# Retention attention on one core: the products across chunks done for two pairs of heads at a time

## Chip, core and metric

The kernel runs on one core of one Trainium2 chip. The metric is the device time in microseconds (us) of one execution; lower is better.

## What is computed

The program is a retention layer followed by two feed-forward layers, all in float32.

```python
# attention: B, H, S, D = 4, 8, 576, 64
scores = scale * (q @ k.T)                     # per batch and head
gamma = 1.0 - 2.0 ** (-5.0 - np.arange(H))
Dmat = np.where(rel >= 0, gamma[:, None, None] ** rel, 0.0)   # rel = row - column
x = (scores * Dmat) @ v                        # -> 2304 tokens x 512
# two layers, 512 -> 2048 -> 512
h = x @ w_in;   g = max(h, 0) + alpha * min(h, 0);   x = g @ w_out
h = x @ w2_in;  g = h * sigmoid(1.702 * h);          out = g @ w2_out
```

## The kernel before

Two heads are worked on together and called a pair: 4 batches times 4 pairs give 16 pairs, numbered 0 to 15 in `PAIRS`. The 64 rows of the first head lie on partitions 0 to 63, those of the second on 64 to 127 (`halves`). The 576 positions are cut into four chunks of 128 and a tail of 64. Because the decay is a power of the distance, the result of a chunk has two parts: a product within the chunk (a masked score matrix times v), and a product across chunks (a decayed 64x64 running state times the queries of the chunk).

The attention is a loop with one round per pair and one more at the end (`for i in range(n_a + 1)`). The program order on every engine is the order of this code; nothing moves instructions later. The PE work of round i is, in this order:

- `a_scores(i)`: k times q per chunk, K = 64 rows, one head on each half of the array's rows; results in `sc`.
- `a_outer(i)`: k times v per chunk, all 128 rows, one head on each half of the array's columns; results in `st`.
- `a_within(j)` with j = i - 1: the masked scores times v, again one head on each half of the columns; results in `av`.
- `a_tail(i)`: the scores of the 64-position tail, 64x64, one head on each of two tiles on the diagonal of the array; results in `st`.
- `a_across(j)`: the states times the queries, 64x64 tiles, one head on each of the two diagonal tiles: three chunks of 128 columns, one of 64, and the "corner" that uses the tail's scores. It adds to `av`.

Beside it the other engines do the following for each pair. DVE: `a_evac(i)` multiplies the two score tiles by a decay table into `r` (L319); `a_sums(i)` makes three small running sums of states (L348, L353, L358); `a_rests` forms the low part of x, for pairs 0 to 7 alone (L91, x<-av). ACT: `a_states(i)` scales `st` into `r` (L251), `a_keys(i+1)` scales the keys in `kts` (L251), and `a_out(j)` copies `av` out (L86, into `x` or `xs`). POOL: `a_queries(i)` scales the queries. SP issues the loads: `a_load(i+4)` at the end of round i fetches the 864 KB of a pair's q, k and v into `ld` (L243), and 256 KB of keys in another layout into `kts` (L245). There are five `ld` buffers, so the load of pair n waits until pair n - 5 has been read for the last time, which is the corner product in `a_across`.

Between these steps the loop also prepares the first layer's weights, from a table of times (`rows`, `at`, `run_to`): for each of the first three blocks of weights two loads of 512 KB on SP (L115), and on DVE a clamp, two bit operations and a subtraction (L123, L126, L133, L140, L91 w<-cv). After the attention come the first layer (L445, L488) and the second (L613).

In PSUM, `av` has two buffers of two banks, `sc` three of one, `st` one.

Of the kernel before, what the change touches and what calls it, by code (L numbers as in the profile page):

```python
# [26 lines left out]
TMP = {"ld": (4, 5, 6, 7, 10), "r": (8, 9), "xs": (12, 13, 14, 15)}  # L27
A0 = 256
# [13 lines left out]
def kernel(  # L42
# [42 lines left out]
    def copy(out, in_):  # L85
        return nc.scalar.activation(out=out, in_=in_, func=ACTF.Copy)  # L86
# [12 lines left out]
    def run_to(time):  # L99
        while events and events[0][0] <= time:  # L100
            _, _, fn, args = events.pop(0)
            fn(*args)
# [122 lines left out]
                at(tick(t + max(d + 2.4, 5.2) + 1.3), b_store, j, i)  # L225


    ld, r_t, k_t, s_t, sc_t, av_t, xs_t = {}, {}, {}, {}, {}, {}, {}

    def tmp(what, i, shape):  # L230
        tags = TMP[what]
        return wp.tile(shape, F32, tag=f"w{tags[i % len(tags)]}", name=what)

    halves = (slice(0, 64), slice(64, 128))
    def kts(i):
        return kts_t[i // 4 % 2][:, i % 4]

    def a_load(i):
        b, p = PAIRS[i]
        t = tmp("ld", i, [128, 1728])  # L240
# [14 lines left out]
        return fade_sb[o, c:c + n]  # L255

    def a_decay():
        dq = aps.tile([128, 1024], F32, tag="av", name="dq", bufs=2)
        for c in range(0, H * 128, 512):
            nc.tensor.matmul(  # L260
                out=dq[:, c:c + 512], lhsT=ones, rhs=fades_sb[:, c:c + 512], start=True, stop=True,
                skip_group_check=True,
            )
        for c in range(0, H * 128, 512):
            copy(fade_sb[:, c:c + 512], dq[:, c:c + 512])

    def a_tables(p):
        def table(o, c0, n, row, key):
# [28 lines left out]
    def a_scores(i, chunks=range(4)):  # L297
# [4 lines left out]
        for j in chunks:  # L302
            for e, o in enumerate(halves):
                mm(t[e][:, j * 128:j * 128 + 128], k[j][o], q[j][o], j == 0, True)

    def a_tail(i):
        q, k = ld[i][0:2]
        for o in halves:
            mm(s_t[i][o, 0:64], k[4][o], q[4][o], i == 0, True)

    def a_outer(i):
        t, v, n = s_t[i], ld[i][2], k_t.pop(i)
        for j in range(4):
            for e, o in enumerate(halves):
                mm(t[o, j * 64 + 64:j * 64 + 128], n[:, j, o], v[:, 2 * j + e], i > 0 and j == 0, True)

    def a_evac(i):
        for e, t in enumerate(sc_t.pop(i)):
            nc.vector.tensor_tensor(  # L319
                out=r_t[i][0][:, e].rearrange("p (j n) -> p j n", j=4),  # L320
                in0=t.rearrange("p (j n) -> p j n", j=4),
                in1=tab_sb[:, PAIRS[i][1], e * 128:e * 128 + 128].rearrange(
                    "p (a n) -> p a n", a=1).to_broadcast([128, 4, 128]),
                op=ALU.mult,
            )

    def a_queries(i):
        behind = latest[0]
        r = tmp("r", i, [128, 2048])
        r_t[i] = (  # L330
            r[:, 0:1024].rearrange("p (e n) -> p e n", e=2), r[:, 1024:1536],
            r[:, 1088:1600].rearrange("p (b n) -> p b n", b=2)[:, :, 0:64], r[:, 1600:2048],
        )
# [27 lines left out]

    def a_within(i):
        v, r = ld[i][2], r_t[i][0]
        t = aps.tile([128, 1024], F32, tag="av", name="av", bufs=2)
        av_t[i] = t, [t[:, A0 + j * 128:A0 + j * 128 + 128] for j in range(4)] + [t[:, A0 + 512:A0 + S]]
        for j in range(4):
            for e, o in enumerate(halves):
                mm(av_t[i][1][j][o], v[:, 2 * j + e], r[:, e, j * 128:j * 128 + 128], j % 2 == 0, True)

    def a_across(i):  # L370
        out, v = av_t[i][1], ld[i][2]
        _, s, _, q = r_t.pop(i)
        for c in range(1, 5):
            s0 = 64 if c == 1 else 192 + c * 64
            for o in halves:
                mm(out[c][o], s[o, s0:s0 + 64], q[o, c * 128 - 128:min(c * 128, 448)], False, True)
        for o in halves:
            mm(out[4][o], v[o, 8], s[o, 0:64], False, True)

    def a_out(i):  # L380
        b, p = PAIRS[i]
        t = av_t.pop(i)[0][:, A0:A0 + S]
        ld.pop(i)
        s0 = 0
        for c in range(2):
            n0, n1 = max(CH[c][0] - b * S, 0), min(CH[c][1] - b * S, S)
            if n0 >= n1:
                continue
            if (0, c, p) not in x_t:
                x_t[0, c, p] = xp[c].tile([128, 2, 512], F32R, tag=f"x{p}", name="x")  # L390
            o = b * S - CH[c][0]
            x = x_t[0, c, p][:, :, n0 + o:n1 + o]
            copy(x[:, 0], t[:, n0:n1])
            rests.append((x, t[:, n0:n1]))
            s0 = n1
        if s0 < S:
            n = i - NP
            if n // 3 not in xs_t:
                xs_t[n // 3] = tmp("xs", n // 3, [128, 3, S])
            copy(xs_t[n // 3][:, n % 3, s0:S], t[:, s0:S])  # L400

    rests = []

    def a_rests():
        while rests:
            x, t = rests.pop(0)
            sub(nc.vector, x[:, 1], t, x[:, 0])

    def a_store(i):
        b, p = PAIRS[i]  # L410
        s0, n = 448 if b == 1 else 0, i - NP
        nc.sync.dma_start(out=x0[b][:, p, s0:S], in_=xs_t[n // 3][:, n % 3, s0:S])


    g_t = {}
# [331 lines left out]

    with tc.manual_schedule():
        kts_t = [wp.tile([128, 4, 512], F32, tag=f"w{n}", name="kts") for n in (3, 11)]
        for t, a in ((fades_sb, fades), (vtab_sb, vtab)):  # L750
            nc.scalar.dma_start(out=t, in_=a)
        nc.vector.memset(wz, 0.0)  # L752
# [19 lines left out]
        a_otab(0)  # L772
        for i in range(n_a + 1):
            j = i - 1
            if i < n_a:
                a_scores(i)
                a_queries(i)
                a_evac(i)
            if i in (1, 2):
                a_tables(i + 1)  # L780
            a_rests()
            run_to(i)
            if i < n_a:
                s_t[i] = aps.tile([128, 512], F32, tag="st", name="st")
                if i == 0:
                    a_tail(i)
                    a_fill(1)
                a_outer(i)
                if i == 0:
                    a_states(i)  # L790
                    a_tables(1)
            if i != 1:
                a_within(max(j, 0))
            if 0 < i < n_a:
                a_tail(i)
                a_states(i)
            if i < n_a:
                a_sums(i)
            if i + 1 < n_a:
                a_keys(i + 1)  # L800
            if i == 0:
                a_otab(1)
# [138 lines left out]
def _layout(q, k, v, moe_w_in, moe_w_out, moe_alpha, moe2_w_in, moe2_w_out):  # L941
# [59 lines left out]
```

## Time and profile before

| | us |
|---|---|
| median of 3 runs | 818.18 (817.46 to 818.82) |
| the profiled execution, its own time | 817.99 |
| its span | 816.3 |
| PE busy in the span | 811.8 |
| DVE busy in the span | 629.1 |
| ACT busy in the span | 461.3 |

The span runs from the first instruction to the last; the execution's own time has 1.7 us more around it. PE is busy for 99% of the span. That does not say that every part of it is at the same limit: the attention is the first 68 us, the rest is the two layers.

### The profile page before, as it was taken

How to read it: one execution, taken by the hardware profiler on the slowest of the kernel's cores; microseconds unless marked ns; L12 is line 12 of the kernel's file. 1: busy time of each engine (PE TensorE's matmuls, PEld its weight loads, DVE VectorE, ACT ScalarE, POOL GpSimd, SP SyncE). 2: the span in 40 equal slices, each digit the busy share in tenths (PEclk: the TensorE clock that was granted, in tenths of full speed). 3: DMA queues.
4: the chain of work that ended last, by engine and by line, in shares of the span. 5: the costliest groups of instructions: out<-in, count | busy, mean ns of one | idle time of the engine just before them, and what ended most of it. 6: DMA issues, size and time to landing. Idle time of an engine off the chain costs nothing.

```text
span 816.3 us, 14024 instructions
## 1 busy us (share of the span) xinstructions
PE 811.8 (99%) x5102; PEld 743.0 (91%) x5102; DVE 629.1 (77%) x1145; ACT 461.3 (57%) x927; POOL 36.6 (4%) x54
## 2 busy tenths in 40 slices
PE   9999999999999999999999999999999999999998
PEld 8988888888888888999888899999999999999998
DVE  6897877786665778687579888699687799677775
ACT  6666655545344544554455766576566666566553
POOL 2330000000001010100100000000000000000000
PEclk9999999999999999999999999999999999999999
DMA  9994734443265665664566553877544986446871
GB/s 348 395 337 158 238 129 154 155 155 129 99 218 183 202 210 185 220 208 155 169 192 194 179 164 110 312 276 275 176 120 139 350 295 226 141 123 208 301 265 70
DMA packets 65722, 166.61 MB, mean 204 GB/s; under 512 B 7155, under 2 KB 32755, under 8 KB 59894
## 3 DMA queue, kind: packets, MB, share of 16 engines
q1 hardware_dynamic: 60896, 148.93, 53.0%
q0 software_dynamic: 4608, 16.78, 7.1%
q8 instruction: 40, 0.66, 0.3%
q14 instruction: 28, 0.23, 0.1%
q10 hardware_dynamic: 150, 0.02, 0.0%
HBM read 128.48 MB, written 37.22 MB: 203 GB/s over the span
## 4 chain that ended last, share of the span: by engine, by line
PE 99%; DVE 0%; issue 0%
PE h L445 24%; PE acc L488 24%; PE acc L613 24%; PE h L613 19%; PE av L287 4%; PE sc L287 2%; PE st L287 2%; PE wps L764 0%; PE dq L260 0%; DVE c L516 0%; DVE wz L752 0%
## 5 line engine op out<-in xcount | busy, mean ns | idle before, releaser
L445 PE MATMUL h<-x,w 128*128 128x512 f32 (+1 forms) x960 | 210.6, 368 | 0.0
L488 PE MATMUL acc<-gsf,w 128*128 128x512 f32 (+1 forms) x960 | 209.8, 368 | 0.0
L86 ACT ACTIVATE gsf<-g 128x384 fp32r<-128x384 f32 (+2 forms) x248 | 132.9, 543 | 116.7 <-DVE g L457 73.8
L445 PEld LDWEIGHTS h<-x,w 128*128 128x128 f32 x960 | 168.1, 189 | 30.8 <-ACT xs L86 0.4
L488 PEld LDWEIGHTS acc<-gsf,w 128*128 128x128 f32 x960 | 168.3, 189 | 30.0
L91 DVE TENSOR_TENSOR gsf<-g,gsf 128x384 fp32r<-128x384 f32 (+2 forms) x248 | 141.3, 578 | 49.0 <-ACT gsf L86 48.4
L457 DVE SCALAR_TENSOR_TENSOR g<-h,nalpha_sb,g 128x512 f32<-128x512 f32 (+1 forms) x80 | 55.6, 695 | 66.8 <-ACT h L456 66.7
L613 PE MATMUL acc<-x,ws 128*128 128x384 f32 x552 | 106.8, 334 | 0.0
L613 PE MATMUL acc<-gsf,ws 128*128 128x384 f32 x576 | 101.3, 334 | 0.0
L613 PEld LDWEIGHTS acc<-gsf,ws 128*128 128x128 f32 x576 | 100.0, 188 | 0.0
L613 PEld LDWEIGHTS acc<-x,ws 128*128 128x128 f32 x552 | 96.7, 188 | 0.0
L613 PE MATMUL h<-x,ws 128*128 128x384 f32 x456 | 90.3, 334 | 0.0
L455 ACT ACTIVATE g<-h 128x512 f32<-128x512 f32 (+1 forms) x80 | 43.8, 548 | 69.9 <-PE h L445 69.9
L613 PEld LDWEIGHTS h<-x,ws 128*128 128x128 f32 x456 | 80.1, 188 | 0.1
L613 PE MATMUL h<-gsf,ws 128*128 128x384 f32 x432 | 76.4, 334 | 0.0
L613 PEld LDWEIGHTS h<-gsf,ws 128*128 128x128 f32 x432 | 75.0, 188 | 0.1
L516 DVE TENSOR_TENSOR tm<-h,tm 128x384 f32<-128x384 f32 x73 | 40.5, 554 | 32.2 <-PE h L613 27.6
L91 DVE TENSOR_TENSOR ws<-rw,ws 128x512 fp32r<-128x512 f32 x96 | 56.9, 615 | 0.0
L516 DVE TENSOR_TENSOR g<-g,g 128x384 f32<-128x384 f32 x93 | 51.4, 552 | 0.7
L86 ACT ACTIVATE ws<-rw 128x512 fp32r<-128x512 f32 x96 | 49.8, 569 | 0.2 <-DMA rw<-rg 0.2
L456 ACT ACTIVATE h<-h 128x512 f32<-128x512 f32 (+1 forms) x80 | 43.9, 549 | 0.0
L119 ACT ACTIVATE cv<-raw 128x1024 f32<-128x1024 f32 x32 | 36.4, 1136 | 6.7 <-DMA raw<-in_w_dram 5.5
(83 smaller groups left out, 712.5 us busy)
## 6 DMA issues: line engine op xcount, KB each, us to landing
ws<-sg SPq DMA_DIRECT2D x42, 1024.0 KB, 6.4
raw<-in_w_dram SPq DMA_DIRECT2D x32, 512.0 KB, 4.9
raw<-in_w_dram POOLq DMA_DIRECT2D x32, 512.0 KB, 5.3
rw<-rg SPq DMA_DIRECT2D x24, 512.0 KB, 3.6
ld<-in_qkv_dram SPq DMA_DIRECT2D x13, 864.0 KB, 7.0
rw<-rg SPq DMA_DIRECT2D x24, 384.0 KB, 3.1
sg<-sums SPq DMA_DIRECT2D x40, 128.0 KB, 2.3
kts<-in_kn_dram SPq DMA_DIRECT2D x16, 256.0 KB, 7.1
```

Of the source, the lines that this page charges most:

```text
L86: return nc.scalar.activation(out=out, in_=in_, func=ACTF.Copy)
L91: latest[0] = eng.tensor_tensor(out=out, in0=a, in1=b.bitcast(F32), op=ALU.subtract)
L119: nc.scalar.activation(out=cvs[key], in_=raws[key][:, :, 1].bitcast(F32), func=ACTF.Abs)
L287: return nc.tensor.matmul(out=out, lhsT=lhsT, rhs=rhs, start=start, stop=stop, skip_group_check=True)
L445: nc.tensor.matmul(out=t, lhsT=w[:, cw, k * 128:k * 128 + 128], rhs=x[:, cx], start=(i == 0), stop=(i == 3 * NK - 1),)
L455: nc.scalar.activation(out=g, in_=t, func=ACTF.Relu)
L456: nc.scalar.activation(out=t, in_=t, func=ACTF.Relu, scale=-1.0)
L457: nc.vector.scalar_tensor_tensor(out=g, in0=t, scalar=nalpha_sb[:, m:m + 1], in1=g, op0=ALU.mult, op1=ALU.add)
L488: nc.tensor.matmul(out=acc[0][d], lhsT=w[:, cw, d * 128:d * 128 + 128], rhs=g[:, cx], start=(m == m0 and i == 0), stop=(m == m1 - 1 and i ...
L516: nc.vector.tensor_tensor(out=out, in0=x, in1=y, op=op)
L613: nc.tensor.matmul(out=out, lhsT=w(cw), rhs=x(cx), start=(start and n == 0), stop=True, skip_group_check=True,)
```

## The change

- `a_across` takes two pairs at once, 2m and 2m+1, and is called in every second round (even i, for pairs i - 2 and i - 1). For odd pairs the output halves are swapped (`side`): the first head's result goes to partitions 64 to 127, the second's to 0 to 63. With that the four heads of two pairs lie on four different 64x64 tiles of the array.
- So that the first layer still sees the right rows, the weight rows of odd 128-row blocks of `w_in` are rolled by 64 when the arrays are laid out.
- PSUM is dealt out anew: `av` is one bank for each of an even and an odd pair (the four chunks), the 64-column tail of the result has its own tile `avt` (one bank for the even pair; the odd pair takes one of the three `sc` banks), and `st` has two banks.
- `a_tail` for pairs 2m and 2m+1 is done in one place, in round 2m. So the tail of an odd pair now reads its `ld` a round earlier than anything did before.
- `a_keys(i+1)` moves ahead of `a_outer(i)`, and so on ACT ahead of `a_states(i)`.
- `a_out` of two pairs follows each `a_across`, with the 64-column tail as a copy of its own. `a_rests` of the even pair stands ahead of `a_evac` in the odd round, that of the odd pair behind it.
- The homes of `r` and `xs` in SBUF are laid out differently, since two more pairs are alive at a time. The number of `ld` buffers stays five, and SP's transfers are the same in the same order.

```diff
+    def side(i, e):
+        return halves[(e + i) % 2]
...
     def a_within(i):
         v, r = ld[i][2], r_t[i][0]
-        t = aps.tile([128, 1024], F32, tag="av", name="av", bufs=2)
-        av_t[i] = t, [t[:, A0 + j * 128:A0 + j * 128 + 128] for j in range(4)] + [t[:, A0 + 512:A0 + S]]
+        t = av_t[i] = aps.tile([128, 512], F32, tag=f"av{i % 2}", name="av")
         for j in range(4):
+            for e in range(2):
+                mm(
+                    t[side(i, e), j * 128:j * 128 + 128], v[:, 2 * j + e],
+                    r[:, e, j * 128:j * 128 + 128], j == 0, True,
+                )
+
+    def a_across(pair):
+        for i, tag, bufs in zip(pair, ("av2", "sc"), (1, 3)):
+            t = aps.tile([128, 512], F32, tag=tag, name="avt", bufs=bufs)
+            av_t[i] = av_t[i], t[:, 0:64]
+
+        def chunk(i, c):
+            s0 = 64 if c == 1 else 192 + c * 64
+            _, s, _, q = r_t[i]
             for e, o in enumerate(halves):
-                mm(av_t[i][1][j][o], v[:, 2 * j + e], r[:, e, j * 128:j * 128 + 128], j % 2 == 0, True)
-
-    def a_across(i):
-        out, v = av_t[i][1], ld[i][2]
-        _, s, _, q = r_t.pop(i)
+                out = av_t[i][1][side(i, e)] if c == 4 else av_t[i][0][side(i, e), c * 128:c * 128 + 128]
+                mm(out, s[o, s0:s0 + 64], q[o, c * 128 - 128:min(c * 128, 448)], c == 4, True)
+
+        def corner(i):
+            for e, o in enumerate(halves):
+                mm(av_t[i][1][side(i, e)], ld[i][2][o, 8], r_t[i][1][o, 0:64], False, True)
+
         for c in range(1, 5):
-            s0 = 64 if c == 1 else 192 + c * 64
-            for o in halves:
-                mm(out[c][o], s[o, s0:s0 + 64], q[o, c * 128 - 128:min(c * 128, 448)], False, True)
-        for o in halves:
-            mm(out[4][o], v[o, 8], s[o, 0:64], False, True)
+            for i in pair:
+                chunk(i, c)
+        for i in pair:
+            corner(i)
+        for i in pair:
+            r_t.pop(i)
...
         for i in range(n_a + 1):
             j = i - 1
+            first = i % 2 == 0
+            done = (i - 2, i - 1) if first and i else ()
             if i < n_a:
                 a_scores(i)
                 a_queries(i)
+                if not first:
+                    a_rests(i - 3)
                 a_evac(i)
...
-            a_rests()
+            if not first:
+                a_rests(i - 2)
             run_to(i)
+            if 0 < i < n_a - 1:
+                a_keys(i + 1)
...
             if i != 1:
                 a_within(max(j, 0))
+            if i == 1:
+                a_tail(1)
+            elif first and 0 < i < n_a:
+                a_tail(i)
+                a_tail(i + 1)
             if 0 < i < n_a:
-                a_tail(i)
                 a_states(i)
             if i < n_a:
                 a_sums(i)
-            if i + 1 < n_a:
-                a_keys(i + 1)
...
-            if i:
-                a_across(j)
-                a_out(j)
+            if done:
+                a_across(done)
+                for n in done:
+                    a_out(n)
...
         wi, wo = np.asarray(wi), np.asarray(wo)
-        wi = wi.reshape(NK, 128, NM, 128).transpose(2, 1, 0, 3).reshape(NM, 128, DM)
+        wi = wi.reshape(NK, 128, NM, 128)
+        if s == "1":
+            wi = np.stack([np.roll(wi[k], 64 * (k % 2), axis=0) for k in range(NK)])
+        wi = wi.transpose(2, 1, 0, 3).reshape(NM, 128, DM)
```

How the rows stand on PE: before, a round in the middle of the attention (`sc` scores, `st<-ld,kts` outer, `av<-r,ld` 64x128 within, `st<-ld` tail, `av<-r` across, and the corner at the end):

```order
L287 MATMUL sc<-ld 128x128 x8
L287 MATMUL st<-ld,kts 64x64 x8
L287 MATMUL av<-r,ld 64x128 x8
L287 MATMUL st<-ld 64x64 x2
L287 MATMUL av<-r 64x128 x6
L287 MATMUL av<-r 64x64 x2
L287 MATMUL av<-r,ld 64x64 x2
```

Now, an odd round and the even one behind it, which together do two pairs:

```order
L297 MATMUL sc<-ld 128x128 x8
L297 MATMUL st<-ld,kts 64x64 x8
L297 MATMUL av<-r,ld 64x128 x8
L297 MATMUL sc<-ld 128x128 x8
L297 MATMUL st<-ld,kts 64x64 x8
L297 MATMUL av<-r,ld 64x128 x8
L297 MATMUL st<-ld 64x64 x4
L297 MATMUL av<-r 64x128 x12
L297 MATMUL avt<-r 64x64 x4
L297 MATMUL avt<-r,ld 64x64 x4
```

The odd round lost its tail and its product across chunks; the even round has both for two pairs.

On DVE, in the rounds of pairs 7 and 8 before (L319 evac, L91 rest, L123 to L140 weights, L348 to L358 sums):

```order
L319 TENSOR_TENSOR r<-sc,tab_sb 128x512 x2
L91 TENSOR_TENSOR x<-av,x 128x448
L123 TENSOR_SCALAR cv<-cv 128x1024
L126 TENSOR_SCALAR cv<-cv 128x1024
L348 SCALAR_TENSOR_TENSOR r<-r,vtab_sb 128x192
L353 SCALAR_TENSOR_TENSOR r<-r,vtab_sb 128x128
L358 TENSOR_TENSOR r<-r,tab_sb 128x64
L319 TENSOR_TENSOR r<-sc,tab_sb 128x512 x2
L91 TENSOR_TENSOR x<-av,x 128x448
L133 SCALAR_TENSOR_TENSOR cv<-raw,cv 128x1024
```

And now, in the same two rounds:

```order
L90 TENSOR_TENSOR x<-av,x 128x448
L337 TENSOR_TENSOR r<-sc,tab_sb 128x512 x2
L90 TENSOR_TENSOR x<-av,x 128x448
L122 TENSOR_SCALAR cv<-cv 128x1024
L125 TENSOR_SCALAR cv<-cv 128x1024
L366 SCALAR_TENSOR_TENSOR r<-r,vtab_sb 128x192
L371 SCALAR_TENSOR_TENSOR r<-r,vtab_sb 128x128
L376 TENSOR_TENSOR r<-r,tab_sb 128x64
L337 TENSOR_TENSOR r<-sc,tab_sb 128x512 x2
L132 SCALAR_TENSOR_TENSOR cv<-raw,cv 128x1024
```

The two rests have gathered in the odd round, one ahead of its evac; the number of instructions on DVE is the same.

## Rows read from the trace of the kernel before

**Rows 1.** The page's busy times (us, share, instructions) and its chain that ended last.
```profile
PE 811.8 (99%) x5102; PEld 743.0 (91%) x5102; DVE 629.1 (77%) x1145; ACT 461.3 (57%) x927; POOL 36.6 (4%) x54
PE h L445 24%; PE acc L488 24%; PE acc L613 24%; PE h L613 19%; PE av L287 4%; PE sc L287 2%; PE st L287 2%; PE wps L764 0%; PE dq L260 0%; DVE c L516 0%; DVE wz L752 0%
```

**Rows 2.** Stretches: length; busy of PE, PEld, DVE, ACT, POOL; clock, DMA share, GB/s.
```profile
20.00:30.00 10.00, 10.00 (x194) 8.92 (x190) 8.42 (x21) 5.68 (x15) 3.51 (x4) 1.00 1.02 417
...
15.22:67.03 51.81, 51.81 (x1002) 46.74 (x996) 47.07 (x99) 32.94 (x73) 16.01 (x14) 1.00 0.91 343
19.00:59.75 40.75, 40.75 (x786) 36.71 (x781) 36.68 (x78) 24.70 (x56) 12.59 (x11) 1.00 0.98 372
```

**Rows 3.** Timeline of PE (start, us, operation, tiles): round 8 and on.
```profile
36.25 1.16 PE L287 MATMUL sc<-ld 64*128 64x128 f32 x16
37.34 0.69 PE L287 MATMUL st<-ld,kts 128*64 128x64 f32 x16
37.86 1.05 PE L287 MATMUL av<-r,ld 128*64 128x128 f32 x16
38.83 0.33 PE L287 MATMUL st<-ld 64*64 64x64 f32 x4
39.00 0.94 PE L287 MATMUL av<-r 64*64 64x128 f32 x16
39.77 0.28 PE L287 MATMUL av<-r,ld 64*64 64x64 f32 x4
39.98 1.16 PE L287 MATMUL sc<-ld 64*128 64x128 f32 x16
```

**Rows 4.** Timeline of DVE: the evac of pair 2, one round, the last sums.
```profile
15.22 1.28 DVE L319 TENSOR_TENSOR r<-sc,tab_sb 128x512 f32<-128x512 f32 x2
...
41.40 1.28 DVE L319 TENSOR_TENSOR r<-sc,tab_sb 128x512 f32<-128x512 f32 x2
42.60 0.61 DVE L91 TENSOR_TENSOR x<-av,x 128x448 fp32r<-128x448 f32 x1
43.13 1.21 DVE L140 SCALAR_TENSOR_TENSOR cv<-raw,cv 128x1024 int32<-128x1024 int32 x1
44.27 0.41 DVE L348 SCALAR_TENSOR_TENSOR r<-r,vtab_sb 128x192 f32<-128x192 f32 x1
...
45.11 1.28 DVE L319 TENSOR_TENSOR r<-sc,tab_sb 128x512 f32<-128x512 f32 x2
...
66.90 0.22 DVE L358 TENSOR_TENSOR r<-r,tab_sb 128x64 f32<-128x64 f32 x1
```

**Rows 5.** Timeline of SP's queue: when loads are issued.
```profile
17.57 0.33 SPq L243 DMA_DIRECT2D ld<-in_qkv_dram  x1
...
18.42 0.43 SPq L115 DMA_DIRECT2D raw<-in_w_dram  x1
21.47 0.33 SPq L243 DMA_DIRECT2D ld<-in_qkv_dram  x1
...
51.75 0.38 SPq L245 DMA_DIRECT2D kts<-in_kn_dram  x1
```

**Rows 6.** The page's loads of pairs over the whole attention: KB, median us to landing.
```profile
ld<-in_qkv_dram SPq DMA_DIRECT2D x13, 864.0 KB, 7.0
```

**Rows 7.** The same by window: loads issued in 17:19, in 21:24, in 51:52.1.
```profile
ld<-in_qkv_dram SPq DMA_DIRECT2D x1, 864.0 KB, 6.2
raw<-in_w_dram SPq DMA_DIRECT2D x1, 512.0 KB, 7.2
...
ld<-in_qkv_dram SPq DMA_DIRECT2D x1, 864.0 KB, 6.3
...
kts<-in_kn_dram SPq DMA_DIRECT2D x1, 256.0 KB, 8.0
```

**Rows 8.** The attention's end: timelines of PE and ACT, and a row of waits.
```profile
67.13 0.99 PE L287 MATMUL av<-r 64*64 64x128 f32 x16
...
68.17 8.79 PE L445 MATMUL h<-x,w 128*128 128x512 f32 x36
...
PEld h L445 <- ACT xs L86: 0.4, 1, 0.4
```

More of the change, by code (lines that the diff above doesn't have):

```diff
@@ L26 @@
 F64_MAX = 2.0 ** 17 * (1 - 2.0 ** -24)
-TMP = {"ld": (4, 5, 6, 7, 10), "r": (8, 9), "xs": (12, 13, 14, 15)}
-A0 = 256
+LOADS = (4, 5, 6, 7, 10)
 BLOCKS = [(0, 0, 0, 3), (0, 1, 0, 8), (0, 0, 3, 11), (0, 1, 8, NM), (0, 0, 11, NM)]
@@ L225, in pair_words, with work, rest_home @@
                 at(tick(t + max(d + 2.4, 5.2) + 1.3), b_store, j, i)
[L228 to L232, printed above, removed]
+    ld, r_t, k_t, s_t, sc_t, av_t = {}, {}, {}, {}, {}, {}
     halves = (slice(0, 64), slice(64, 128))
+    def side(i, e):
+        return halves[(e + i) % 2]
+    def work(i):
+        a, b = r_home[i % 2], r_home[i % 3]
+        c = 1024 if i % 3 < 2 else 0
+        return a[:, 0:1024], b[:, c:c + 960]
+    def rest_home(i):
+        n = i - 2 * NP
+        if n < 0:
+            n += NP
+            return xs_home[n // 2][:, 1728 + n % 2 * 128:1856 + n % 2 * 128]
+        return xs_home[n // 3][:, n % 3 * S:n % 3 * S + S]
     def kts(i):
@@ L239, in a_load @@
         b, p = PAIRS[i]
-        t = tmp("ld", i, [128, 1728])
+        t = wp.tile([128, 1728], F32, tag=f"w{LOADS[i % len(LOADS)]}", name="ld")
         cuts = {0: (0, 512, 1152, 1728), 1: (0, 1152, 1728), 2: (0, 1152, 1728)}.get(i, (0, 1728))
@@ L257, in a_decay @@
     def a_decay():
-        dq = aps.tile([128, 1024], F32, tag="av", name="dq", bufs=2)
-        for c in range(0, H * 128, 512):
+        dq = [aps.tile([128, 512], F32, tag="st", name="dq", bufs=2) for _ in range(2)]
+        for n, t in enumerate(dq):
             nc.tensor.matmul(
-                out=dq[:, c:c + 512], lhsT=ones, rhs=fades_sb[:, c:c + 512], start=True, stop=True,
+                out=t, lhsT=ones, rhs=fades_sb[:, n * 512:n * 512 + 512], start=True, stop=True,
                 skip_group_check=True,
             )
-        for c in range(0, H * 128, 512):
-            copy(fade_sb[:, c:c + 512], dq[:, c:c + 512])
+        for n, t in enumerate(dq):
+            copy(fade_sb[:, n * 512:n * 512 + 512], t)
     def a_tables(p):
@@ L304, in a_scores @@
                 mm(t[e][:, j * 128:j * 128 + 128], k[j][o], q[j][o], j == 0, True)
+    k_done = set()
     def a_tail(i):
         q, k = ld[i][0:2]
+        if i not in s_t:
+            s_t[i] = aps.tile([128, 512], F32, tag="st", name="st", bufs=2)
         for o in halves:
-            mm(s_t[i][o, 0:64], k[4][o], q[4][o], i == 0, True)
+            mm(s_t[i][o, 0:64], k[4][o], q[4][o], i not in k_done, True)
     def a_outer(i):
+        new = i not in s_t
+        if new:
+            s_t[i] = aps.tile([128, 512], F32, tag="st", name="st", bufs=2)
         t, v, n = s_t[i], ld[i][2], k_t.pop(i)
+        k_done.add(i)
         for j in range(4):
             for e, o in enumerate(halves):
-                mm(t[o, j * 64 + 64:j * 64 + 128], n[:, j, o], v[:, 2 * j + e], i > 0 and j == 0, True)
+                mm(t[o, j * 64 + 64:j * 64 + 128], n[:, j, o], v[:, 2 * j + e], new and j == 0, True)
     def a_evac(i):
@@ L328, in a_queries @@
         behind = latest[0]
-        r = tmp("r", i, [128, 2048])
+        c, r = work(i)
         r_t[i] = (
-            r[:, 0:1024].rearrange("p (e n) -> p e n", e=2), r[:, 1024:1536],
-            r[:, 1088:1600].rearrange("p (b n) -> p b n", b=2)[:, :, 0:64], r[:, 1600:2048],
+            c.rearrange("p (e n) -> p e n", e=2), r[:, 0:512],
+            r[:, 64:576].rearrange("p (b n) -> p b n", b=2)[:, :, 0:64], r[:, 512:960],
         )
@@ L363, in a_within, with pieces @@
         v, r = ld[i][2], r_t[i][0]
[L364 to L365 removed]
+        t = av_t[i] = aps.tile([128, 512], F32, tag=f"av{i % 2}", name="av")
         for j in range(4):
[L367 to L378 removed]
+            for e in range(2):
[10 more added lines that the diff above has]
+            _, s, _, q = r_t[i]
+            for e, o in enumerate(halves):
+                out = av_t[i][1][side(i, e)] if c == 4 else av_t[i][0][side(i, e), c * 128:c * 128 + 128]
[3 more added lines that the diff above has]
+                mm(av_t[i][1][side(i, e)], ld[i][2][o, 8], r_t[i][1][o, 0:64], False, True)
+        for c in range(1, 5):
+            for i in pair:
[4 more added lines that the diff above has]
+            r_t.pop(i)
     def a_out(i):
         b, p = PAIRS[i]
[L382 removed]
+        t = av_t.pop(i)
         ld.pop(i)
+        def pieces(n0, n1):
+            if n0 < 512:
+                yield t[0][:, n0:min(n1, 512)], n0, min(n1, 512)
+            if n1 > 512:
+                yield t[1][:, max(n0, 512) - 512:n1 - 512], max(n0, 512), n1
         s0 = 0
@@ L391, in a_out, with a_rests @@
             o = b * S - CH[c][0]
-            x = x_t[0, c, p][:, :, n0 + o:n1 + o]
-            copy(x[:, 0], t[:, n0:n1])
-            rests.append((x, t[:, n0:n1]))
+            for f, m0, m1 in pieces(n0, n1):
+                x = x_t[0, c, p][:, :, m0 + o:m1 + o]
+                copy(x[:, 0], f)
+                rests.setdefault(i, []).append((x, f))
             s0 = n1
         if s0 < S:
[L397 to L406, printed above, removed]
+            h = rest_home(i)
+            for f, m0, m1 in pieces(s0, S):
+                copy(h[:, m0 - s0:m1 - s0], f)
+    rests = {}
+    def a_rests(i):
+        for x, t in rests.pop(i, ()):
             sub(nc.vector, x[:, 1], t, x[:, 0])
@@ L410, in a_store @@
         b, p = PAIRS[i]
-        s0, n = 448 if b == 1 else 0, i - NP
-        nc.sync.dma_start(out=x0[b][:, p, s0:S], in_=xs_t[n // 3][:, n % 3, s0:S])
+        nc.sync.dma_start(out=x0[b][:, p, 448 if b == 1 else 0:S], in_=rest_home(i))
     g_t = {}
@@ L749 @@
         kts_t = [wp.tile([128, 4, 512], F32, tag=f"w{n}", name="kts") for n in (3, 11)]
+        r_home = [wp.tile([128, 2048], F32, tag=f"w{n}", name="r") for n in (8, 9, 15)]
+        xs_home = [wp.tile([128, 2048], F32, tag=f"w{n}", name="xs") for n in (12, 13, 14)]
         for t, a in ((fades_sb, fades), (vtab_sb, vtab)):
@@ L780 @@
                 a_tables(i + 1)
-            a_rests()
+            if not first:
+                a_rests(i - 2)
             run_to(i)
+            if 0 < i < n_a - 1:
+                a_keys(i + 1)
+            if i == 0:
+                a_tail(0)
+                a_fill(1)
             if i < n_a:
-                s_t[i] = aps.tile([128, 512], F32, tag="st", name="st")
-                if i == 0:
-                    a_tail(i)
-                    a_fill(1)
                 a_outer(i)
-                if i == 0:
-                    a_states(i)
-                    a_tables(1)
+            if i == 0:
+                a_states(i)
+                a_tables(1)
             if i != 1:
                 a_within(max(j, 0))
+            if i == 1:
[3 more added lines that the diff above has]
+                a_tail(i + 1)
             if 0 < i < n_a:
-                a_tail(i)
                 a_states(i)
@@ L798 @@
                 a_sums(i)
-            if i + 1 < n_a:
-                a_keys(i + 1)
             if i == 0:
+                a_keys(1)
                 a_otab(1)
             run_to(i + 0.25)
-            if i:
-                a_across(j)
-                a_out(j)
+            if done:
+                a_across(done)
+                for n in done:
+                    a_out(n)
             if i in (1, 2):
```

## Prediction

> **What bounds the kernel now.** I read the chain that ended last first: PE holds 99% of it, and `av`, `sc` and `st`, the attention's results, are 8% together [rows 1]. So a microsecond that PE saves in the attention is a microsecond of the time, as long as nothing else takes its place; that is the question for the stretches. From 20 to 30 us PE has no free time, DVE is 84% busy, and the DMA engines' share is 1.02 at 417 GB/s [rows 2]. From the evac of pair 2 to the last sums (15.22 to 67.03) DVE works 47.07 of 51.81 us, and from 19.00 to 59.75 the transfers take 0.98 of the engines [rows 2]. PE comes first, and two others stand close behind it. That decides the sum.
>
> PE's timeline gives a round's groups from start to start [rows 3]: scores 1.09 us, outer 0.52, within 0.97, tail 0.17, across 0.98 (39.00 to 39.98, chunks 0.77 and corner 0.21), together 3.73. In the chunks 16 records of 0.27 us or so fit into 0.77 us: two tiles run side by side.
>
> **The change, step by step: PE.** The products across chunks of two pairs go to four tiles. If all four run side by side, two pairs take the 0.98 us of one, and each of eight calls saves 0.98: 7.8 us. Bounds: 0, if only two tiles ever run together; 7.8, if four do. Nearest are the chunk products themselves and the outer products, which run two tiles that share all rows of the array at 16 records in 0.52 us [rows 3]. I take the full 7.8, since I find no row in which a second tile slows a first one. The second tail put beside the first adds two steps of 64 columns; the outer group does eight such steps in 0.52, so two cost 0.13 where a tail by itself costs 0.17 [rows 3]: 0.04 saved seven times, 0.3 us. PE by itself would so need 8.1 us less, and two rounds would take 2 x 3.73 - 0.98 - 0.04 = 6.4 us.
>
> One rule of the Trainium skill speaks against this. *TensorE: Matmul & The Clock Gate*, Part 3, says that a weight load overlaps matmuls in flight only where the row group differs; of four 64x64 tiles two always share their rows. By it the second pair would wait and PE would gain the 0.3 us of the tails alone. The outer group's two tiles share all 128 rows and run 16 records with their weight loads in 0.52 us, which the trace could not show if each load waited for the other tile's 0.22 us matmul; so the trace does not agree where I can see it. It remains a rival.
>
> **DVE.** It gets the same 99 instructions between the evac of pair 2 and the last sums, 47.07 us of work [rows 2], in another order. Its start at 15.22 [rows 4] stays: round 1 has no product across chunks any more, but the sums of pair 1 and the tables stand ahead on DVE. So the last sums cannot end before 15.22 + 47.07 = 62.3; now they end at 67.1 [rows 4]. Waits come on top. A round costs DVE 1.20 for the evac and 0.84 for the sums, a weight step 1.14, a rest 0.53 (start to start, 41.40 to 45.11) [rows 4]; a rest of pairs 0 to 3 covers 576 columns for 448, an estimate of 0.68. Two rounds then hold: rounds 3 and 4, and 5 and 6, 4.08 + 2 x 0.68 = 5.4 us of work, below PE's 6.4, so DVE waits 1.0 each time, 2.0 in all; rounds 7 and 8, 9 and 10, 4.08 + 1.06 + 2.28 = 7.4, above PE's 6.4, so PE waits; rounds 11 to 14, 4.08 + 2.28 = 6.4, even. The last sums so end near 62.3 + 2.0 = 64.3. Behind them come the rest of the last product across chunks, at least the corner's 0.21 and at most the whole 0.98 [rows 3]; the first chunks need only `a_states`, so I take 0.5. The attention ends near 64.8 instead of at 68.17 [rows 8]: **3.4 us less**, not 8.1. Bounds for this step: no waits give 62.5, 5.7 us less; the 4.74 us that DVE idles now (51.81 - 47.07) give 67.5, 0.7 less.
>
> **Loads.** SP's transfers are the same in the same order, but the load of an odd pair n waits for the corner of pair n - 5, now done with its neighbour's one round later, and `a_tail(n)` wants it a round earlier, in round n - 1. From the corner to that tail lie two times scores, outer and within and one tail: 2 x 2.58 + 0.17 = 5.3 us. Loads take 7.0 us to land [rows 6], which would be too long. But these 7.0 are queueing: a load issued at 17.57 lands at 23.8, weights issued at 18.42 at 25.6, the next load issued at 21.47 at 27.8 [rows 5, 7]. Each lands 2.2 us (864 KB) behind the one ahead, whenever it was issued. In the changed kernel the odd load comes first of two; the queue ahead of it holds what is left of the batch before, and I expect it to land within 5.3 us, or late by a few tenths that fall into the waits counted above. The last keys land at 51.75 + 8.0 = 59.75 [rows 5, 7]. From 19.00 on the queue never ran dry, at 372 GB/s [rows 2]; the same bytes at 417 GB/s would be there 4.4 us earlier, at 55.4. I take the middle, 57.6. `a_keys(15)` now stands ahead of `a_states(14)` on ACT, so DVE's sums of pair 14, due 64.3 - 0.84 - 1.14 - 1.20 - 0.84 = 60.3, wait for these keys, with about 1.4 us of ACT between: landing by 58.9 costs nothing, at 59.75 it costs 0.9.
>
> **The rest.** ACT has twelve more copies of 64 columns; it is 5.7 of 10 us busy [rows 2], and they hide there. At the attention's end PE now waits 0.4 us in the second product of the first layer for ACT's last copy [rows 8]. The changed kernel's copies come even later, but into a bank that only the third product needs, one product or 2.9 us later (8.79 / 3): 0.4 us saved. The first layer's weight work on DVE and ACT keeps its distance to the end of the attention, so everything behind it moves up whole. The rolled weight rows are laid out ahead of the launch and cost nothing.
>
> Sum: 817.99 - 3.4 - 0.4 = **814.2 us**, against the profiled execution's own 817.99, which lies 0.2 below the median of the runs.
>
> **Rivals.**
> - *Tiles that share rows do not overlap.* PE keeps its 0.98 us per pair. Against it stand the outer products [rows 3]; for it, that no row has four tiles at work. Then the 0.3 of the tails and the 0.4 at the end stay: 817.3, no change. 0.10. That is what the page's rule would give.
> - *Odd loads come late: slower.* If the six odd loads from pair 5 to 15 keep their 7.0 us, with 0.3 us of issue each costs PE 7.0 + 0.3 - 5.3 = 2.0 us, 12 in all against 8.1 + 0.4 gained: 821.5. It turns slower when they take over 6.4 us on average (6 x 1.4 = 8.5). For it: the DMA share of 0.98 and the weights that come between. Against it: the 2.2 us spacing. 0.12.
> - *More waits on DVE, little gain.* In the odd round `a_within` waits for a buffer that a rest frees, and the rest for ACT's copies of that pair. If DVE idles as much as now, 0.7 + 0.4 are left: 816.9. 0.12.
> - *DVE and loads bind nothing:* 817.99 - 8.1 - 0.4 = 809.5. DVE's 47.07 us of work stand against it. 0.03.
> - My forecast, with 812.0 to 816.2 as its own range (DVE without waits at the low end; the loads late by 0.9 and another microsecond of waits at the high end): 0.63.
>
> **How the numbers follow.** About 0.2%, 1.6 us, is what a measurement of this kernel can tell from no change. Faster takes the forecast, the free case and half of the case of little gain (it ends at 816.4): 0.63 + 0.03 + 0.06, and a little for loads that are late less often, 0.74. Within 0.2%: the tiles that do not overlap and the other half, 0.15. Slower 0.11. The range reaches from 811.9 to 817.3: below it lies the free case, above it the late loads and part of the no-overlap case, some 0.2.
>
> **What would show it.** Right: `av<-r` records of four tiles starting almost together, chunks and corner of two pairs in about 1.0 us; the attention's last group ending near 64.8; DVE almost without idle time from round 7 on, and PE waiting there for `r` (evac or sums) or for a rest in `av`. Wrong: across groups of 1.9 us for two pairs (no overlap); PE waiting for `ld` at the `st<-ld` records of even rounds, 1 us or more each (late loads); DVE idle above 4 us in the stretch. The prediction would also be wrong if the first layer then waited for weights, which come from the same queue and the same DVE.

## The result and the profile after

The changed kernel takes **825.66 us** (median; 824.79 to 826.30) beside 818.35 us for the kernel before (four runs, where the table above has three): a ratio of 1.0085, 95% interval 1.0073 to 1.0098. It is slower by 7 us, where I forecast 814.2, 3.8 us less. The range (811.9 to 817.3) does not hold it.

The page after: busy times and the chain that ended last, which answer to [rows 1].
```profile
PE 809.5 (98%) x5102; PEld 738.4 (90%) x5102; DVE 627.5 (76%) x1145; ACT 462.8 (56%) x939; POOL 36.4 (4%) x54
PE 85%; DMA 7%; DVE 4%; ACT 2%; issue 1%; SPq 0%; DVEq 0%; ACTq 0%
```
The chain was 99% PE; now transfers hold 7% of it and PE 85%. By tile they are the weights of the first layer (4%), the loads of the pairs (2%) and the keys (1%). So the first thing to ask is when these are late, and who waits. The stretches of the changed kernel (columns as in [rows 2]) say when:
```profile
18.00:18.50 0.50, 0.50 (x14) 0.50 (x12) 0.15 (x1) 0.50 (x2) 0.00 (x0) 1.00 0.09 33
...
20.00:30.00 10.00, 8.95 (x170) 7.87 (x172) 7.45 (x19) 5.74 (x16) 3.43 (x3) 1.00 0.93 344
...
15.25:74.88 59.63, 49.82 (x1006) 42.61 (x1004) 46.36 (x100) 32.44 (x81) 15.96 (x14) 1.00 0.83 299
```
From 20 to 30 us PE is now idle for 1.05 us and 344 GB/s flow instead of 417 [rows 2]. At 18.0 the DMA engines stand almost still, at 33 GB/s. From the evac of pair 2 to the last sums (15.25 to 74.88) DVE has about as much work as before (46.36 us, then 47.07), in 59.63 us: 13.3 us idle instead of 4.7.

SP's queue and, by window, the landing of the loads issued at 17.79 and 18.71 (answers to [rows 5, 7]):
```profile
17.79 0.33 SPq L253 DMA_DIRECT2D ld<-in_qkv_dram  x1
...
18.71 0.37 SPq L253 DMA_DIRECT2D ld<-in_qkv_dram  x1
...
25.98 0.33 SPq L253 DMA_DIRECT2D ld<-in_qkv_dram  x1
```
```profile
ld<-in_qkv_dram SPq DMA_DIRECT2D x1, 864.0 KB, 6.8
ld<-in_qkv_dram SPq DMA_DIRECT2D x1, 864.0 KB, 8.5
```
Two buffers come free together at the end of an even round, two loads start together, with the keys and a block of weights beside them (I call that a bunch), and no further load starts for 7 us. PE's timeline, from the end of round 4 to round 7 (answers to [rows 3]; in brackets idle time and what ended it):
```profile
24.70 0.27 PE L297 MATMUL st<-ld 64*64 64x64 f32 x2 [0.52 <-DMA ld<-in_qkv_dram]
...
25.84 1.16 PE L297 MATMUL sc<-ld 64*128 64x128 f32 x16
...
32.05 0.39 PE L297 MATMUL st<-ld 64*64 64x64 f32 x6
32.23 0.33 PE L297 MATMUL av<-r 64*64 64x128 f32 x2
...
33.32 1.16 PE L297 MATMUL sc<-ld 64*128 64x128 f32 x16
35.23 1.08 PE L297 MATMUL st<-ld,kts 128*64 128x64 f32 x16 [0.75 <-ACT kts L261]
37.56 1.09 PE L297 MATMUL av<-r,ld 128*64 128x128 f32 x16 [1.25 <-DVE x L90]
```
Two things are to be seen. The change does on PE what it says: two tails and the products across for two pairs take 32.05 to 33.32, 1.27 us, where before took 2 x (0.17 + 0.98) = 2.30 [rows 3]. And it gains nothing, since PE waits between the groups. What it waits for in round 7 is an outer group without keys, and a product within without a rest. Behind both stands ACT, in the same stretch:
```profile
33.66 1.13 ACT L118 ACTIVATE cv<-raw 128x1024 f32<-128x1024 f32 x1 [4.42 <-DMA raw<-in_w_dram]
34.69 0.89 ACT L261 ACTIVATE kts<-kts,vtab_sb 128x256 f32<-128x256 f32 x2
35.49 0.50 ACT L261 ACTIVATE r<-st,vtab_sb 128x320 f32<-128x320 f32 x1
```
and DVE waits 3.83 us for that last row:
```profile
36.02 0.42 DVE L366 SCALAR_TENSOR_TENSOR r<-r,vtab_sb 128x192 f32<-128x192 f32 x1 [3.83 <-ACT r L261]
```
(L118 is ACT's first step on a block of weights; it stands in ACT's order between keys, states and copies.) The waits of engines from 0 to 80 us (total, times, longest):
```profile
DVE r L366 <- ACT r L261: 13.1, 6, 3.8
ACT kts L261 <- DMA kts<-in_kn_dram: 12.9, 8, 3.2
ACT cv L118 <- DMA raw<-in_w_dram: 9.6, 3, 4.4
...
PE st L297 <- DMA ld<-in_qkv_dram: 2.7, 4, 0.9
```
In order of time, the transfers of 6 us and more on the chain that ended last, from 15 to 75 us:
```profile
17.79 6.77 DMA ld<-in_qkv_dram
...
26.85 6.79 DMA raw<-in_w_dram
...
43.43 8.21 DMA raw<-in_w_dram
...
61.33 6.67 DMA raw<-in_w_dram
```
Only the first is the load of a pair. The later ones are weights out of the same bunches, with ACT's step on them, the keys and the states behind.

The attention ends at 75.39 us, 7.2 later than in [rows 8]; another 0.9 is lost behind it.

### The profile page after: what moved, and what is told of

Its sections match the earlier page's. It is cut to its first block, busy times and chain, and to the rows that moved or that the text cites. A ratio compares the mean times of both kernels' runs of the same rounds, so it can differ in the third digit from the quotient of the medians.

```text
span 824.4 us, 14022 instructions
## 1 busy us (share of the span) xinstructions
PE 809.5 (98%) x5102; PEld 738.4 (90%) x5102; DVE 627.5 (76%) x1145; ACT 462.8 (56%) x939; POOL 36.4 (4%) x54
## 4 chain that ended last, share of the span: by engine, by line
PE 85%; DMA 7%; DVE 4%; ACT 2%; issue 1%; SPq 0%; DVEq 0%; ACTq 0%
PE acc L652 24%; PE acc L527 21%; PE h L484 21%; PE h L652 19%; DMA raw<-in_w_dram 4%; DMA ld<-in_qkv_dram 2%; PE av L297 1%; DMA kts<-in_kn_dram 1%; DVE cv L139 1%; DVE g L496 1%; DVE cv L132 1%; ACT cv L118 0%; DVE w L90 0%; ACT kts L261 0%; DVE gsf L90 0%
## 5 line engine op out<-in xcount | busy, mean ns | idle before, releaser
L118 ACT ACTIVATE cv<-raw 128x1024 f32<-128x1024 f32 x32 | 36.1, 1128 | 16.2 <-DMA raw<-in_w_dram 14.5
```

Source lines behind the costliest of these rows:

```text
L118: nc.scalar.activation(out=cvs[key], in_=raws[key][:, :, 1].bitcast(F32), func=ACTF.Abs)
```

## Experiments

The theory: loads that are issued two at a time leave the DMA queue empty in between; keys, weights and odd loads then come late, and ACT, which works in order, hands that on to DVE and PE. The rivals: ACT's new order alone, the early tails, or the new homes of the tiles. Times are medians; each ratio is to the kernel before, run on the same chip.

**A sixth load buffer (e1_six).** Tile `w2` is free until round 16.
```diff
-LOADS = (4, 5, 6, 7, 10)
+LOADS = (4, 5, 6, 7, 10, 2)
```


> The changed kernel with a sixth buffer for the loads of a pair (in SBUF that stands empty until the third block of weights is formed), so that no odd load waits for a product across chunks of the same round. Theory A (the release of the buffers every second round makes the loads arrive late, and PE, ACT and DVE wait for them in turn): PE no longer waits for a load, a pair of rounds falls from about 8.2 us to under 7.2, and the time comes to 812 to 817 us. Rival B (the new order on ACT and DVE, keys ahead of states and a rest ahead of the evac, is what costs): 822 to 826 us.

Measured 817.9 us, 0.9996 (0.9985 to 1.0007): all of the loss comes back, and no gain; 0.9 us above theory A's range and 4 below rival B's. Two rounds take 7.5, 6.4, 7.7 and 7.8 us there (from the scores at 16.70 us on), where I had expected under 7.2. The stretches show a queue that no longer runs dry; from 17.0 to 19.5 us the changed kernel had 139 GB/s:
```profile
17.00:19.50 2.50, 1.94 (x40) 1.69 (x38) 2.31 (x7) 2.42 (x9) 0.00 (x0) 1.00 1.02 412
20.00:30.00 10.00, 10.00 (x220) 8.99 (x220) 8.71 (x22) 5.53 (x14) 4.53 (x4) 1.00 1.02 416
```

**One round for each pair (e12_each_round).** Five buffers, all else of the change, but chunk products, copies and rests of one pair a round.
```diff
-            done = (i - 2, i - 1) if first and i else ()
+            done = (i - 1,) if i else ()
-                if not first:
-                    a_rests(i - 3)
-            if not first:
-                a_rests(i - 2)
+            a_rests(i - 2)
```


> Five load buffers and everything else of the change, but each pair's chunk products, its output copies and its rests come in a round of their own, so a load buffer comes free every round. Theory A (the loss comes from releases that come two at a time): the loads stand one a round again, the DMA queue stays above 400 GB/s between 20 and 40 us, and the time is 817 to 819.5. Theory B (something else of the change, the homes of the tiles, the swapped halves or the place of the keys and tails, costs the time): 822 to 826.

820.04 us, 1.0021 (1.0012 to 1.0031). Of the 7.3 us lost, 5.6 come back without a sixth buffer, by issuing loads one at a time (22.51, 26.25, 29.98 in its trace); some 1.7 remain, and the time is just above what I expected. The other sign that I had put down, more than 400 GB/s from 20 to 40 us, did not come: it is 378, with the engines' share at 1.00, where the kernel before has 398.

**The rivals, with five buffers.** The chunk products one pair after the other (e2_two_tiles), the odd pair's tail in its own round (e4_own_tail), the keys behind the states on ACT (e5_keys_back), and ACT's first step on weight block 0 a round later (e14_abs_only).
```diff
 e2  -for c in range(1, 5): for i in pair: chunk(i, c)
     +for i in pair: for c in range(1, 5): chunk(i, c)
 e4  -a_tail(i); a_tail(i + 1)    (even rounds, before the states)
     +a_tail(i)                   (each round)
 e5  a_keys(i + 1) moved from before a_outer(i) to behind a_sums(i)
 e14 -(2.8, 5.75, 7.0, ...        +(2.8, 6.75, 7.0, ...
```


> The changed kernel with the chunk products of one pair ahead of those of the other, so that only two tiles are at work at a time; all else as changed. It measures what four tiles give. If PE were what the attention waits for, 8 x 0.75 = 6 us more, 831 to 832 us. By theory A (loads set the pace) most of that is on the loads' path too, since the corner that releases a buffer comes 0.75 us later in each call: 829 to 832 us. If four tiles had given nothing: 825 to 826 us and the same 1.1 us for the products of two pairs.

> The changed kernel with the tail of an odd pair back in its own round, so that its load is wanted a round later; the buffers' release stays late. Theory A: the 2.7 us in which PE waits for a load at the tails go, but the keys of the odd pair are still wanted in the round before, so only 1 to 3 us come back: 823 to 825 us. Rival B: 825 to 826 us, no change.

> The changed kernel with the scaling of the next pair's keys back behind the states on ACT. Theory A: the loads are as late as before, but ACT no longer holds the states of pair i back until the keys of pair i + 1 have landed: 1 to 4 us come back, 821 to 824.5 us. Rival B, if it is this order alone that costs: under 818 us.

> The changed kernel with its five load buffers, and only ScalarE's first step on weight block 0 one round later. Theory A (the releases two at a time set the period by themselves, and ScalarE's waits for weight transfers are only where the lateness of the queue shows): 823.5 to 826, hardly any change. Theory B (ScalarE's waits for the weights, 9.6 us in three pieces in the changed kernel, with keys and states queued behind them, are a cause of their own): 821 to 823.

Measured: e2 825.59 us (ratio 1.0083, 1.0064 to 1.0102), e4 824.93 (1.0083, 1.0060 to 1.0106), e5 824.5 (1.0069, 1.0051 to 1.0088) and e14 824.28 (1.0075, 1.0062 to 1.0087). None brings back more than about 1 us, and the intervals do not tell that from nothing. For e2 theory A had 829 to 832 us, and that was wrong. Its products take 1.51 us for two pairs (32.35 to 33.86 us), 0.4 more than in the changed kernel, and the time shows none of it. So with a dry queue it made no clear difference whether PE works on two tiles or four, nor which of the late things ACT or PE meets first. (A part of what e4, e5 and e14 gain may be hidden by a lower clock, last section.)

**What limits it with six buffers.** Keys back (e6_six_keys); chunk products one pair after the other (e3_six_two_tiles); the later step on block 0 (e8_six_abs); and, leaving out DVE's integer steps on the first three weight blocks (`w_clamp`, `w_top`, `w_low`), e9_six_noprep. The edits are those above; e9 returns at the head of the three functions.

> Sixth load buffer, and the scaling of the next round's keys on ScalarE stands behind the states again, as before the change. Theory A (ScalarE's order: keys that wait for their transfer hold back the states and so VectorE's sums): 816 to 817.5, a part of the about 2 us that VectorE's sums wait for ScalarE in the six-buffer kernel. Theory B (the wait is only passed on: the keys are then late for the outer products and TensorE waits there): 817.5 to 818.5.

> With the sixth load buffer the changed kernel took 817.9 us. Here, beside the sixth buffer, the chunk products of two pairs stand one pair after the other, so only two 64x64 tiles are at work at a time; over seven pairs of rounds that is about 0.9 us of TensorE each (1.96 against 1.08 to 1.11 us), 6 us in all. Theory A (what sets the period is now VectorE, ScalarE's order and the DMA queue, not TensorE): 817.5 to 819.5, since TensorE had about 1 us to spare in each pair of rounds. Theory B (TensorE is what the six-buffer kernel waits for): 822 to 824.

> Sixth load buffer, and ScalarE's first step on weight block 0, which waited 2.86 us for its transfer in the six-buffer kernel with keys and states queued behind it, comes one round later. Theory A (that wait is on the path): 815.5 to 816.8. Theory B (VectorE, busy 9.7 of 10 us between 40 and 60 us, makes it up later and loses the weight steps' room in rounds 5 and 6): 817.5 to 818.5.

> Sixth load buffer; the integer steps of VectorE on the first three weight blocks (12 instructions, about 10.9 us by the trace of the six-buffer kernel) are left out, so those blocks' weights hold other numbers. If VectorE bounds the attention stage of the six-buffer kernel: it ends near 62 instead of 66.4 us, 812 to 814.5. If the DMA queue (416 GB/s until the last load) bounds it: 816 to 817.5.

Measured: e6 817.42 us (0.9994, 0.9985 to 1.0003); e3 818.09 (0.9999, 0.9990 to 1.0008); e8 **816.73** (0.9980, 0.9971 to 0.9989); e9 815.27 (0.9964, 0.9950 to 0.9978). e6 and e3 cannot be told from e1, so neither ACT's order nor the four tiles show in the time here. e8 fits theory A: ACT no longer stops for block 0, and the attention ends at 64.91 where e1 had 66.35. e9 falls between: with 10.9 us of DVE's work gone its attention still ends only at 65.62, 0.73 us earlier than in e1, while its span is 1.8 us shorter; the rest of its gain lies behind the attention. And DVE now waits for ACT instead:
```profile
DVE r L373 <- ACT r L268: 10.5, 9, 3.0
ACT cv L118 <- DMA raw<-in_w_dram: 8.0, 3, 3.6
```
So DVE is not alone in setting the six-buffer pace; these waits, and 416 GB/s from 16 to 45 us in that run, point to the transfers beside it. (Its granted clock reads 0.95 of 2.4 GHz from 16 us on, with PE hardly idle; 36 products still take 8.46 us.)

**With both edits.** Keys back as well (e10_six_abs_keys); chunk products one pair after the other (e13_six_abs_two); weight block 1 two rounds later (e11_six_abs_raw1); the same two edits on the kernel before (e7_before_six_abs).
```diff
 e11 -(7.2, 9.75, 11.0, 12.0, 13.0, 13.25, 14.0)
     +(9.2, 11.75, 12.0, 13.0, 13.9, 14.25, 15.0)
```


> The changed kernel with the sixth buffer, the later step on block 0 (these two alone: 816.73 us) and the keys behind the states on ScalarE. Theory A (the keys' waits for their transfers, 6.0 us in six pieces, hold back the states and so VectorE, which bounds the stage): 815.5 to 816.5. Theory B (these waits end before VectorE would have come to the sums, of which it waits only 3.0 us in five pieces): 816.4 to 817.4.

> The changed kernel with the sixth buffer and the later step on block 0 (816.73 us), and with the chunk products of two pairs one pair after the other, on two tiles at a time, which adds about 6 us of TensorE. Theory A (VectorE, with 9.3 to 9.7 of 10 us busy between 30 and 60 us, bounds the stage and TensorE has about 5 us to spare in it): 816.5 to 818. Theory B (TensorE bounds it): 820 to 822.5.

> The changed kernel with the sixth buffer and the later step on block 0, and weight block 1 fetched and worked on two rounds later, behind two more loads. Theory A (the DMA queue, at 385 to 418 GB/s until 50 us, sets when the last loads land): the attention stage ends up to 1.5 us earlier, 815.5 to 816.7. Theory B (VectorE sets it, and now has block 1's steps in the last rounds beside those of block 2): 817 to 818.5.

> The kernel before with the same two edits that made the changed kernel faster than it (a sixth load buffer, and ScalarE's first step on weight block 0 one round later). Theory A (the chunk products on four tiles are worth something once neither the loads nor that step holds them back): 817.5 to 819, no change, since TensorE is busy throughout the attention stage of before. Theory B (the gain came from the two edits and not from the change): 816 to 817.2.

Measured: e10 816.46 us (0.9976, 0.9967 to 0.9985), no clear step from e8; e13 818.89 (1.0011, 1.0002 to 1.0020); e11 817.43 (1.0000, 0.9989 to 1.0010), a loss, whose cause I did not follow; e7 818.13 (1.0001, 0.9993 to 1.0010). e8 against e13 is what it is worth here to alternate two pairs on four tiles, 2.2 us by the medians and 2.5 by the ratios, and e7 says that the two edits by themselves are worth nothing to the kernel before. e13 fell between my theories, and its price was too high as well: one pair after the other takes 1.48 us for both, not 1.96. PE's timeline in e13:
```profile
30.56 0.45 PE L297 MATMUL st<-ld 64*64 64x64 f32 x8
30.85 0.89 PE L297 MATMUL av<-r 64*64 64x128 f32 x16
...
32.33 1.16 PE L297 MATMUL sc<-ld 64*128 64x128 f32 x16
```
Here 30.56 to 32.33 answers to 1.27 us on four tiles: 0.50 more, seven times 3.5, of which its attention (67.05 against 64.91) shows 2.1. So PE has some time to spare in e8, but not 3.5 us.

**Where the gain of e8 goes.** Its attention ends 3.26 us earlier than in [rows 8], its span is 1.7 shorter. Three rows of its timelines, of ACT and PE:
```profile
86.86 1.12 ACT L118 ACTIVATE cv<-raw 128x1024 f32<-128x1024 f32 x1 [4.08 <-DMA raw<-in_w_dram]
```
```profile
90.48 3.00 PE L527 MATMUL acc<-gsf,w 128*128 128x512 f32 x12 [0.80 <-DVE os L548]
...
116.16 2.60 PE L484 MATMUL h<-x,w 128*128 128x512 f32 x10 [0.47 <-DVE w L90]
```
The weights of the first layer did not move up with it. ACT stops for block 5's transfer, the activation behind it is late, and so are DVE's copies of the sums that PE waits for. By the starts of the same products, e8 leads the kernel before by 3.59 us at 86.80, by 2.51 from 93.32 to 112.36, by 2.01 at 118.60 and by 1.89 at 326.90. So the wait at 90.48 costs 1.1 us of the lead and the one at 116.16 another 0.5. e15_six_abs_abs5 lets that step come a third of a product step later; e16_before_all has all three edits on the kernel before.
```diff
-[t + d for d in (-1.6, 0.0, 0.5, ...
+[t + d for d in (-1.6, 0.35 if m == 5 else 0.0, 0.5, ...
```


> The changed kernel with the sixth buffer and the later step on block 0 (816.73 us), and ScalarE's first step on weight block 5, which waits 4.08 us for its transfer at 82.8 us with the activations queued behind it, about a third of a step of the product later. Theory A (that wait gives back a part of the gain: TensorE's 0.80 us wait at 89.7 us hangs on the copy of the sums behind it): 815.7 to 816.3. Theory B (the weight steps are late by themselves and TensorE then waits for a block of weights instead): 816.5 to 818.

> The kernel before with the three edits (sixth buffer, later steps on blocks 0 and 5). TensorE waits for nothing there in the attention stage, and not at the place behind it either: 817.5 to 819 by both theories; below 817 the edits would be worth something without the change.

Measured: e15 **815.64 us**, 0.9972 (0.9963 to 0.9981), and e16 820.80, 1.0029 (1.0020 to 1.0039). In e15's trace the product at 89.66 starts without a wait, and the lead on the kernel before is still 3.45 us at 100.54, where e8 had 2.51 left. The profiled execution, one of its slower ones at 817.04, then loses it at other places (3.01 at 321.60, 0.94 at 604.87). The intervals of e15 and e8 overlap, and by the ratios 0.7 us lie between them, not 1.1, so that step is not shown; that e15 is faster than the kernel before is. On the kernel before the third edit does harm: PE waits 2.2 us for a weight block near 118 us. That is neither of the two outcomes I had put down.

## Why the prediction was wrong

- **What bounds the kernel before: right.** PE was the bound, with DVE and the transfers close behind.
- **PE's saving: right in sum.** 2.30 - 1.27 = 1.03 us for two rounds, against 0.98 + 0.04; of it the products across gave 0.87 (1.96 to 1.09, 32.23 to 33.32) and the tails 0.16. The Trainium skill's rule (*TensorE: Matmul & The Clock Gate*, Part 3), that a weight load overlaps matmuls in flight only where the row group differs, spoke against this. The trace does not agree: products on four tiles, of which two always share their rows, take 1.09 us for two pairs. My own reading, "two tiles run side by side" because 16 records of 0.27 us fit into 0.77 us, did not follow from those rows: on the whole array, the first layer's records, 0.39 us each, also start every 0.23 us (36 in 8.29 us in e8). That the time for two pairs nearly halved is what shows the overlap.
- **Loads: this step failed.** From "Each lands 2.2 us (864 KB) behind the one ahead, whenever it was issued" I had the odd load arrive within 5.3 us or a few tenths late, at no cost. I put nothing down for the keys and weights that are issued in the same bunch, but for the last keys. The rows did not bear the spacing out: two loads issued 3.90 us apart landed 4.0 us apart, 6.2 and 6.3 us after their issue [rows 5, 7]. They also came from a queue that was never empty. With two releases every other round and five buffers it ran dry (33 GB/s at 18 us), and a load issued into the nearly empty queue still took 6.8 us, with the other transfers of its bunch beside it. Five of the six odd loads took 6.8, 5.2, 6.6, 6.1 and 6.5 us by window; for the sixth the trace gives no landing. From release to release runs a loop. Its first turn is issue, landing, the odd tail that the change puts right ahead of the products across, those products: 17.63 to 25.84 is 8.2 us, where I had 6.4. Later turns go through the weights of a bunch and ACT, as the chain above has it. That the releases are the cause, e1 and e12 show: a buffer more brings back all of the loss, releases one at a time 5.6 of 7.3 us. e4, which takes the tail out of the loop and gains nothing clear, fits that keys and weights of the same bunch close it as well.
- **The rival of late odd loads** was nearest, with 821.5, but not by its own mechanism. The five odd loads average 6.2 us, less than the 6.4 at which it turned slower, and PE's waits for `ld` come to 2.7 us in the trace, not 12. The larger part came through ACT: 12.9 us of waits for keys and 9.6 for weights, with the states behind them, and so 13.1 us on DVE. I had put `a_keys` ahead of `a_states` on the path for the last pair alone, and ACT's steps on the weights nowhere. e5 and e14 each move one of these steps and bring back about 1 us at most.
- **DVE: the size was right, the waits were not.** Work of 46.4 us in the stretch, against 47.07 forecast; idle 13.3 us, against 2.0. With the releases mended, e8 has this account nearly as forecast: attention's end at 64.91 (64.8), but in part by luck: the stretch starts 1.0 us earlier and has 3.7 us of idle time, not 2.0:
```profile
14.20:64.38 50.18, 46.80 (x1000) 40.98 (x1001) 46.48 (x100) 33.06 (x81) 16.00 (x14) 1.00 0.91 360
```
- **"Everything behind it moves up whole": failed too**, and in e8 it costs about half the gain by itself. In e8 the second product of the first layer starts 8.29 us behind the first, against 8.62 before: 0.33 us saved for the 0.4 forecast at the attention's end. Then the first layer's weight work, which did not come earlier, gives back 1.6 of the 3.59 us at the two waits shown. That the first layer might wait for weights I had named as a sign of being wrong, without a price.

Not settled: the 1.7 us that e12 stays behind the kernel before, and the cause of e11's loss. For e12 the record has a hint: its five executions with a mean clock of 0.997 or 0.998 took 820.0 to 821.3 us, the six others had a median of 819.0. Whether the lower clock costs that time or only goes with longer waits is not shown; the profiled execution, at 818.53, is one of the fast ones.

## What to carry to other kernels

When work is taken in pairs, look at what its end releases: here releases that came two at a time needed a buffer more to keep the transfers flowing, and a landing time read from a queue that is never empty says nothing of one that is. On an engine that works in order, each step that waits for a transfer has a price that its own wait does not show: all that stands behind it. And a saved microsecond moves the time only as far as the next stage's own supply moves with it.

## What the runs showed of the hardware

Transfers that are issued close together share the engines, more than they follow one another. In the changed kernel the load issued at 17.79, when almost nothing else was under way, took 6.8 us. In these 6.8 us the engines moved 310 GB/s, an estimate of 2.1 MB, of which its own 864 KB are 0.88 MB; so over 1 MB of what was issued behind it went through before it had landed. At 417 GB/s its own bytes alone would have been 2.1 us. The second load of the bunch took 8.5 us. The products of one pair overlap with those of the next even when the code puts the chunk products of one pair first: 1.48 us for two pairs in e13, where two calls in different rounds took 1.96 [rows 3].

The long waits also cost TensorE's clock. In e4, after steady work until 32 us, PE works 0.25 us between 32 and 34 us, and then the granted clock stands at the lower of its two levels, 1.2 GHz (0.50 of 2.4), while PE works again (all of the time from 38 to 41 us); at about 41 us it rises. Stretches of e4, and a group of products within at either level from its PE timeline:
```profile
32.00:34.00 2.00, 0.25 (x5) 0.05 (x2) 0.00 (x0) 0.95 (x1) 0.00 (x0) 1.00 1.04 412
...
38.00:40.00 2.00, 2.00 (x20) 1.55 (x18) 1.92 (x5) 0.57 (x2) 0.00 (x0) 0.50 1.00 410
...
42.00:44.00 2.00, 2.00 (x60) 1.76 (x58) 2.00 (x3) 0.81 (x2) 0.31 (x1) 1.00 0.06 16
```
```profile
36.95 1.98 PE L297 MATMUL av<-r,ld 128*64 128x128 f32 x16 [0.81 <-DVE x L90]
...
41.70 1.05 PE L297 MATMUL av<-r,ld 128*64 128x128 f32 x16
```
With the outer group before (1.51 us, later 0.69) and the scores behind (2.00, later 1.16) that is 2.6 us more of PE in one gap. e5 and e14 show the same near 35 and 38 us. The changed kernel's own profiled run kept the full clock throughout; its other runs have a mean of 0.995 to 0.996, so they seem to have such gaps too, and its times do not differ by it (824.79 to 826.30).
